# Queries of two chunks loaded as runs of eight tokens, and four re-orderings, in a fused linear-attention and feed-forward kernel

## The chip, the cores and the metric

The kernel runs on one core of a Trainium2 chip. The metric is the device time of one execution in microseconds (us), lower is better. Runs of the kernel before took 651.63 us (median of three; 650.90 and 653.96 are the other two). One more execution was recorded by the hardware profiler: it took 652.51 us, of which 650.7 us lie between its first and its last instruction (the span).

The engines named below are TensorE (PE for its matmuls, PEld for its weight loads), VectorE (DVE), ScalarE (ACT), GpSimd (POOL) and SyncE (SP). SP and POOL matter here mostly as queues from which DMA transfers are issued, in order.

## The reference

Two blocks in sequence, all in float32 (the inputs `moe_w_in`, `moe_w_out` arrive as 64-bit floats and are converted in the kernel):

```python
# attention: B=4, H=8, S=768, D=64, blocks of 64 tokens
for b in range(nb):
    intra = (qb @ kb.T * Dmask) @ vb
    inter = (qb * lam_pow) @ kv_state
    out[:, :, sl] = intra + inter
    kv_state = lam_block * kv_state + (kb * rev_pow).T @ vb
x = out.transpose(0, 2, 1, 3).reshape(3072, 512)
# feed-forward: d_ff = 2048
h = x @ w_in
g = h - tanh(h)
return g @ w_out
```

## The kernel before

**Groups and chunks.** The 768 tokens are cut into six groups `g` of 128 tokens; a group has four chunks `(g, b)`, one for each batch entry. For each group the kernel computes attention for its four chunks, then the first product `x @ w_in` with tanh (called "up", in four units `u` of 512 columns), then the second product (called "down"). Both products go by seven-product block schemes, the later ones twice nested, so they need sums and differences of weight blocks, called factors. Attention of the next group is woven between the products of the current one.

**Group 0, where the weights arrive too.** SP issues the loads of q, k and v and of the raw weights in one order. `load_natural` (lines 150 to 162) loads a chunk of q as `[token, head, d]` on 128 partitions, in pieces of 256 bytes (64 floats of one head). `att_transpose` (383) turns it on PE into a PSUM bank (`tp`), four 128x128 transposes for q and four for k, and copies each bank out (`qt`, `kt`) with one instruction, on ACT, or on DVE for k of chunks 2 and 3 of group 0. `first_scores` (409) makes eight score matmuls in two PSUM banks (`sp`) and masks them on DVE into `ss`; `first_decay` (421) scales k on DVE; `first_state` (454) makes the products `kv`; `first_out` (458) multiplies `ss` with v into two banks (`op`), from which `copy_xt` fills `xt`, the input of the first up-product (`h`, line 1044). All these PSUM tiles rotate through four banks with the tag "att". `weights` converts one raw weight block (`round_block`, lines 326 to 342: three ACT instructions at 337 to 339, then two DVE instructions at 341 and 342), and issues the loads of later blocks as it goes.

The order of group 0 and of the start of group 1 is written out by hand (lines 1108 to 1204). `tied(True, op)` and `keep_in_program_order` hold an instruction at its written place on its engine; the others are placed by a scheduler. The list `turns` (1163) weaves up-products of units 2 and 3 with conversions and with the attention of group 1; in its first entry one conversion stands in the middle of the up-product, ahead of `att_qd`, whose product `qd` (line 406) the next matmuls of PE (`op`, line 522) read. Then `down_first` (line 1074, tile `acc`) reads `s24`, sums made on DVE by `sums_late` (lines 1083, 1084), while DVE also builds factors (`sums_out`, 303; `sums_fine`, 321) and POOL issues their writes to DRAM.

**Group 1** (`second_units`, 1251). `pieces(g, at)` looks up in a table what attention work of the next group is done at this place; `att_scores` for chunks 0 and 1 stands under key 1. Its keys come from `turn_block` (line 373), a DVE transpose. `inner_weights` writes factors to the DRAM tensor `fine_in`.

**Groups 2 to 5** (`later_units`, 1268). The weight blocks of the twice nested products are streamed from the DRAM tensor `fine` through a ring of seven tiles `wb` (`piece`, 822; issued by POOL at line 843). In group 2 the last fourteen blocks of `fine` are still missing. `fine_factors(n)` (870), a generator for n = 1 and 2, loads four quarters of a factor (`f`, line 878), issues three DRAM-to-DRAM copies (880), and then, at each further step, one DVE difference (`hold`, shown at line 919) and the write of its result (885). `up` drives the steps of n = 2 at the tanh of the units and columns listed at line 680; `later_units` finishes the rest at line 1293.

Of the kernel before, what the change touches and what calls it, by code (L numbers as in the profile page):

```python
# [24 lines left out]
def kernel(  # L25
# [119 lines left out]

    raw, late = {}, {}
    chunks = [(g, b) for g in range(NG) for b in range(B)]
    at = {"loaded": 0}

    def load_natural(g, b, names):  # L150
        for name, src, bufs in (("q", q, 2), ("k", k, 4), ("v", v, 4)):
            if name in names:
                x = (qpool if name == "q" else io).tile([128, H, D], F32, name=f"{name}_nat", tag=name, bufs=bufs)
                if name == "q" or g == 0:
# [227 lines left out]

    def att_transpose(g, bs):
        for b in bs:
            load(g * B + b + 1)
            t = raw[g, b]
            qt = work.tile([128, NP, BLK], F32, name="qt", tag="qt")
            kt = work.tile([128, NP, BLK], F32, name="kt", tag="kt")
            for dst, x in ((qt, "q"), (kt, "k")):
                if g >= GB:  # L390
                    turn_block(dst, t[x + "b"])
# [17 lines left out]
    def first_scores(b):  # L409
        qt, kt, _ = tr[0, b]  # L410
        sp = [bank("sp", "att", 4).rearrange("s (p i) -> s p i", p=NP) for _ in range(2)]
        for p in range(NP):
            for j in range(2):
                tied(True, nc.tensor.matmul(out=sp[j][:, p, :], lhsT=kt[ts(j, 64), p, :], rhs=qt[ts(j, 64), p, :],
                                            start=True, stop=True))
# [3 lines left out]
        sc[0, b] = ss  # L419

    def first_decay(b):
        kp = raw[0, b]["k"].rearrange("s (p j) d -> s p j d", j=2)
        tied(True, nc.vector.tensor_tensor(kp, kp, bwd0, op=AL.mult))
# [34 lines left out]
    def first_out(bs):  # L458
        ops, dst = out_banks()
        for n, b in enumerate(bs):  # L460
            ss, vn = sc.pop((0, b)), raw[0, b]["v"]
# [5 lines left out]
        copy_xt(0, bs[0] // 2, ops)  # L467

    def score_products(g, b, tags):
# [183 lines left out]
    def up(g, u, n, wait=False, inside=False):  # L653
# [21 lines left out]
        def finish(c, src):  # L675
            th = work.tile([128, 2, HB], F32, name="th", tag="th")
            tied(g == 0, nc.scalar.activation(th, src, AF.Tanh))  # L677
            if g >= GI:
                pieces(g, ("t", u, c))
                if (u, c) in ((2, 12), (3, 12), (3, 22)):  # L680
                    next(made[g, 2], None)
# [186 lines left out]
    made = {}  # L868

    def fine_factors(n):  # L870

# [3 lines left out]
        for i in range(2):  # L875
            for j in range(2):
                t.append(late["pool"].tile([128, NU, 128], F32, name="f2", tag="sums", bufs=4))
                tc.keep_in_program_order(nc.gpsimd.dma_start(out=t[-1], in_=f[:, :, i, ts(j, 128)]))
        for x, i, j in ((0, 0, 0), (1, 1, 0), (2, 1, 1)):
            tc.keep_in_program_order(nc.gpsimd.dma_start(out=to[x], in_=f[:, :, i, ts(j, 128)]))  # L880
        yield
# [225 lines left out]

    for b in P0:
        att_transpose(0, (b,))
        first_decay(b)  # L1110
        first_scores(b)
    first_state(P0)
    half = up_plain(0, (11, 12))
    att_transpose(0, (2,))
    first_decay(2)
    weights(1)
    first_out(P0)
    first_scores(2)
    next(half)
# [4 lines left out]
    first_decay(3)  # L1124
    first_scores(3)
    next(half)
    first_state(P1)
    weights(KI + 1)
    first_out(P1)
    sums = first_sums()  # L1130
# [14 lines left out]
    for n in (2, 6, 5, 7):  # L1145
# [3 lines left out]
        if n == 6:  # L1149
# [12 lines left out]
    load(2 * B)  # L1162
    turns = [(2, (11, 21), 1, 1, (), ((att_transpose, 1, P0), (att_qd, 1, P0), (sums_in, 0))),
             (2, (12,), 0, 2, (), ((att_read, 1, P0), (att_scores, 1, P0, ("att", "att", "ya", "yb")))),
# [42 lines left out]
    def pieces(g, at_):  # L1207
# [43 lines left out]
    def second_units(g):  # L1251
        for u in range(NU):
            for n in (2, 6, 5, 7, 1, 4, 3):
# [137 lines left out]
```

## Time and profile before

| what | us |
|---|---|
| median of three runs | 651.63 |
| the profiled execution | 652.51 |
| its span | 650.7 |
| PE busy in the span | 639.8 |
| DVE busy | 497.8 |
| ACT busy | 239.2 |
| POOL busy | 225.4 |

The granted TensorE clock is at full speed in all forty slices of the span. The DMA engines moved 140.45 MB. Busy times by stage, from the view by windows:

| stage, us of the span | PE busy | DVE busy | ACT busy | DMA share |
|---|---|---|---|---|
| 0 to 25 (attention of group 0) | 21.63 | 16.44 | 11.06 | 0.99 |
| 25 to 61 | 35.97 | 30.62 | 28.59 | 0.86 |
| 61 to 127 (weights, factors) | 65.05 | 60.11 | 41.71 | 0.90 |
| 127 to 300 (groups 1 and half of 2) | 172.32 | 139.00 | 52.28 | 0.84 |
| 300 to 312 (products of group 2 begin) | 9.62 | 9.11 | 2.03 | 1.01 |
| 312 to 450 | 137.64 | 108.43 | 40.70 | 0.76 |
| 450 to 650.7 | 197.55 | 134.12 | 62.84 | 0.54 |

A DMA share is the mean busy share of sixteen DMA engines; it can pass 1 where packets overlap. Instructions on one engine run in order, so an engine's time line is read from top to bottom; a bracket behind a row gives the idle time ahead of it and what ended it. Matmul ends are modelled, so that the start-to-start distance of matmuls says more than their durations.

### The profile page before, as it was taken

The page shows a single profiled execution, that of the slowest core. Times are in us where ns is not written, and L with a number is a line of the kernel's source. Part 1 is how long each engine was busy: PE and PEld are TensorE (multiplying, and loading weights), DVE is VectorE, ACT ScalarE, POOL GpSimd, SP SyncE. Part 2 cuts the span into 40 slices and gives each one's busy share as a digit, 9 for nine tenths or more (in the row PEclk, how much of TensorE's full clock was granted, in tenths as well). Part 3 has the DMA queues.
Part 4 walks back from the last instruction along what each step waited for, and adds up shares of the span by engine and source line. Part 5 has one row for each costly group of instructions (what it writes and reads, how often), then busy time and mean ns, then how long its engine had stood idle before and what let it go on. Part 6 is the DMA issues. An engine that isn't in the chain of part 4 may idle for free.

```text
span 650.7 us, 14789 instructions
## 1 busy us (share of the span) xinstructions
PE 639.8 (98%) x5792; PEld 588.9 (90%) x5792; DVE 497.8 (77%) x902; ACT 239.2 (37%) x490; POOL 225.4 (35%) x392
## 2 busy tenths in 40 slices
PE   8999999999999999999999999999999999999998
PEld 7888888888888999888899988999988999988997
DVE  5879997987876967888868777878777878356583
ACT  3787773513322124442122353122344212444110
POOL 2001248782113554243555100646211456300440
PEclk9999999999999999999999999999999999999999
DMA  9979888999468877999979765778683587610582
GB/s 201 272 203 224 228 262 287 327 318 275 128 160 219 264 241 218 236 294 247 289 239 305 177 132 136 261 241 292 206 177 99 166 289 256 212 35 1 161 283 75
DMA packets 108789, 140.45 MB, mean 216 GB/s; under 512 B 64048, under 2 KB 81584, under 8 KB 108720
## 3 DMA queue, kind: packets, MB, share of 16 engines
q0 software_dynamic: 29840, 97.54, 47.1%
q1 hardware_dynamic: 78736, 41.96, 27.3%
q8 instruction: 46, 0.75, 0.5%
q14 instruction: 23, 0.19, 0.1%
q10 hardware_dynamic: 144, 0.00, 0.0%
HBM read 117.18 MB, written 23.86 MB: 217 GB/s over the span
## 4 chain that ended last, share of the span: by engine, by line
PE 70%; issue 10%; DMA 8%; DVE 7%; POOL 3%; SPq 1%; ACT 0%; POOLq 0%; DVEq 0%; ACTq 0%
PE y L961 15%; PE y L669 14%; PE zw L961 11%; PE z L669 5%; PE w L669 5%; PE y L767 4%; PE h L1044 3%; PE z L767 2%; DMA wb<-fine 2%; DMA fine<-f 2%; PE kv L449 1%; PE sp L486 1%; PE op L536 1%; DMA fine<-wt 1%; SPq L161 1%
## 5 line engine op out<-in xcount | busy, mean ns | idle before, releaser
L843 POOL DMA_DIRECT2D wb<-fine x217 | 117.1, 540 | 219.4 <-PE y L961 112.1
L961 PE MATMUL y<-wb,g 128*128 128x128 f32 x624 | 81.3, 276 | 0.6 <-DMA wb<-fine 0.5
L964 ACT ACTIVATE q<-y 128x128 f32<-128x128 f32 x108 | 30.0, 278 | 138.0 <-PE y L961 138.0
L961 PEld LDWEIGHTS y<-wb,g 128*128 128x128 f32 x624 | 75.3, 192 | 1.5 <-DVE ss L493 0.6
L961 PE MATMUL zw<-wb,g 128*128 128x128 f32 x416 | 55.2, 276 | 0.7 <-DMA wb<-fine 0.7
L961 PEld LDWEIGHTS zw<-wb,g 128*128 128x128 f32 x416 | 50.6, 192 | 1.0 <-PE y L961 0.6
L677 ACT ACTIVATE th<-g 128x512 f32<-128x512 f32 x42 | 26.5, 630 | 55.7 <-DVE g L700 20.8
L669 PE MATMUL y<-xt,w 128*128 128x256 f32 x200 | 46.9, 380 | 0.0
L1044 PE MATMUL h<-xt,w 128*128 128x256 f32 x192 | 44.1, 383 | 0.2 <-DVE w L342 0.2
L682 DVE TENSOR_TENSOR g<-g,th 128x512 f32<-128x512 f32 x42 | 29.0, 691 | 17.7 <-ACT th L677 17.5
L669 PEld LDWEIGHTS y<-xt,w 128*128 128x128 f32 x200 | 37.6, 190 | 5.1 <-ACT g L709 0.2
L1044 PEld LDWEIGHTS h<-xt,w 128*128 128x128 f32 x192 | 35.6, 190 | 5.7 <-DVE w L342 0.9
L669 PE MATMUL w<-xt,w 128*128 128x256 f32 x168 | 40.5, 383 | 0.0
L669 PE MATMUL z<-xt,ws 128*128 128x256 f32 x168 | 39.7, 379 | 0.0
L669 PE MATMUL y<-tt,w 128*128 128x256 f32 x160 | 38.1, 381 | 0.0
L669 PE MATMUL y<-tt,ws 128*128 128x256 f32 x160 | 38.1, 380 | 0.0
L669 PEld LDWEIGHTS z<-xt,ws 128*128 128x128 f32 x168 | 31.9, 190 | 4.3
L669 PEld LDWEIGHTS w<-xt,w 128*128 128x128 f32 x168 | 31.0, 190 | 4.5 <-ACT w L640 0.5
L961 PE MATMUL y<-wb,s 128*128 128x128 f32 x248 | 32.8, 275 | 1.5 <-DMA wb<-fine 1.5
L669 PEld LDWEIGHTS y<-tt,w 128*128 128x128 f32 x160 | 30.1, 190 | 4.3 <-DVE g L691 0.2
L669 PEld LDWEIGHTS y<-tt,ws 128*128 128x128 f32 x160 | 30.0, 190 | 3.9
L961 PE MATMUL zw<-wb,s 128*128 128x128 f32 x248 | 33.0, 276 | 0.0
(221 smaller groups left out, 1370.1 us busy)
## 6 DMA issues: line engine op xcount, KB each, us to landing
wb<-fine POOLq DMA_DIRECT2D x217, 256.0 KB, 3.8
fine<-f POOLq DMA_DIRECT2D x24, 256.0 KB, 4.7
wb<-fine_in POOLq DMA_DIRECT2D x24, 256.0 KB, 4.1
raw<-in_moe_w_out_dram POOLq DMA_DIRECT2D x10, 512.0 KB, 5.5
q_blk<-in_q_dram SPq DMA_DIRECT2D x32, 128.0 KB, 4.4
k_blk<-in_k_dram SPq DMA_DIRECT2D x32, 128.0 KB, 5.2
wb<-factors POOLq DMA_DIRECT2D x16, 256.0 KB, 4.5
raw<-in_moe_w_in_dram SPq DMA_DIRECT2D x7, 512.0 KB, 5.9
```

Of the source, the lines that this page charges most:

```text
L161: tc.keep_in_program_order(nc.sync.dma_start(out=x[rows, hs:hs + NP], in_=part.rearrange("h s d -> s h d")))
L449: tied(True, nc.tensor.matmul(out=kv[ts(j, 64), n, p, :], lhsT=kd[:, 2 * p + j, :], rhs=vn[:, 2 * p + j, :], start=n == 0 and p == 0, stop ...
L486: tied(True, nc.tensor.matmul(out=dst, lhsT=keys(p, j, late_), rhs=qt[ts(j, 64), p, rows], start=True, stop=True))
L536: tied(True, nc.tensor.matmul(out=dst(n, p, j)[:, HF:BLK], lhsT=vn[:, 2 * p + j, :], rhs=ss[:, j, p % 2, 1 + p // 2, :], start=first and n ...
L669: tied(g == 0, nc.tensor.matmul(out=t[:, m, :], lhsT=wt[:, kt, ts(m, 128)], rhs=x[:, kt, :], start=first and m == 0 and kt == 0, stop=kt = ...
L677: tied(g == 0, nc.scalar.activation(th, src, AF.Tanh))
L682: tied(g == 0 or g >= GI and inside, nc.vector.tensor_tensor(dst(c), src, th, op=AL.subtract))
L767: tied(True, nc.tensor.matmul(out=dst[:, ts(u, 128)], lhsT=a, rhs=b, start=x in (1, 2, 5) and u == 0, stop=True, skip_group_check=True))
L843: nc.gpsimd.dma_start(out=t.rearrange("p m c -> p (m c)"), in_=fine[TWICE.index(n_), SLOT.index(x_)].rearrange("p u c -> p (u c)"))
L961: tied(True, nc.tensor.matmul(out=dst, lhsT=a[:, u, :], rhs=wb[:, ts(u, 128)], start=x in begins and u == 0, stop=u == NU - 1, skip_group_ ...
L964: nc.scalar.activation(keep, dst, AF.Copy)
L1044: tied(u == 0 or u == 2 and cs[0] == 11, nc.tensor.matmul(out=hm[c][:, m, :], lhsT=w1[u][:, i, a, ts(m, 128)], rhs=xt[0, t][:, i, :], star ...
```

## The change

1. Chunks 0 and 1 of group 0 load q as runs of eight tokens: a partition holds eight consecutive tokens of one head, 2 KB in one piece. The transposes then take two tokens at a time, and four ACT copies of 64 partitions by 256 elements, with gaps in what they read and write, put the result in the layout of `qt`.
2. In the written order of group 0 the scores of chunk 0 are split in halves around the transposes of k of chunk 1, q of chunk 1 is transposed ahead of them, and the outputs of chunks 0 and 1 are parted by the transposes of k of chunk 2.
3. The conversion in the first entry of `turns` moves behind `att_qd`.
4. In group 1 the scores of chunks 0 and 1 for group 2 get places of their own, a little later.
5. The three DRAM-to-DRAM copies of each factor move from group 2 into group 1 (`fine_copies`), and the steps of n = 2 are driven from earlier places; the clean-up at the end of `later_units` goes.

```diff
+    RUNS = ((0, 0), (0, 1))
...
+                if name == "q" and (g, b) in RUNS:
+
+                    rows = src[b, 0, 0:BLK, :]
+                    rows = bass.AP(tensor=rows.tensor, offset=rows.offset, ap=[[8 * D, BLK // 8], [S * D, H], [1, 8 * D]])
+                    tc.keep_in_program_order(nc.sync.dma_start(out=x, in_=rows))
...
+    def runs_transpose(dst, x):
+
+        tp = bank("tp", "att", 4).rearrange("d (i c) -> d i c", i=4)
+        for i in range(4):
+            tied(True, nc.tensor.transpose(out=tp[:, i, :], in_=x[:, 2 * i:2 * i + 2, :], identity=ident))
+        dst = dst.rearrange("d p (t i e) -> d e i t p", i=4, e=2)
+        tp = tp.rearrange("d i (t p j) -> d j i t p", p=NP, j=2)
+        for j in range(2):
+            for e in range(2):
+                tied(True, nc.scalar.activation(dst[ts(j, 64), e], tp[ts(e, 64), j], AF.Copy))
...
         for p in range(NP):
+            if p == NP // 2:
+                yield
             for j in range(2):
...
-                if (u, c) in ((2, 12), (3, 12), (3, 22)):
+                if (u, c) in ((3, 11), (2, 12), (2, 21), (3, 12)):
                     next(made[g, 2], None)
...
+    def fine_copies(n):
+        f = factors[XAT[FACT[n][1]]].rearrange("p (u i) c -> p u i c", i=2)
+        for x, i, j in ((0, 0, 0), (1, 1, 0), (2, 1, 1)):
+            tc.keep_in_program_order(nc.gpsimd.dma_start(out=fine[TWICE.index(n)][x], in_=f[:, :, i, ts(j, 128)]))
...
-        for x, i, j in ((0, 0, 0), (1, 1, 0), (2, 1, 1)):
-            tc.keep_in_program_order(nc.gpsimd.dma_start(out=to[x], in_=f[:, :, i, ts(j, 128)]))
         yield
...
-    for b in P0:
-        att_transpose(0, (b,))
-        first_decay(b)
-        first_scores(b)
+    att_transpose(0, (0,))
+    first_decay(0)
+    att_transpose(0, (1,), "q")
+    scores = first_scores(0)
+    next(scores)
+    att_transpose(0, (1,), "k")
+    every(scores)
+    first_decay(1)
+    every(first_scores(1))
     first_state(P0)
     half = up_plain(0, (11, 12))
-    att_transpose(0, (2,))
+    att_transpose(0, (2,), "q")
+    outs_ = first_out(P0)
+    next(outs_)
+    att_transpose(0, (2,), "k")
     first_decay(2)
     weights(1)
-    first_out(P0)
-    first_scores(2)
+    every(outs_)
+    every(first_scores(2))
...
-    turns = [(2, (11, 21), 1, 1, (), ((att_transpose, 1, P0), (att_qd, 1, P0), (sums_in, 0))),
+    turns = [(2, (11, 21), 0, 1, (), ((att_transpose, 1, P0), (att_qd, 1, P0), (weights, 4 * KI + 1), (sums_in, 0))),
...
-            table.update({0: [(att_transpose, h, P0)], 1: [(att_scores, h, P0), (att_qd, h, P0)],
+            table.update({0: [(att_transpose, h, P0)], 1: [(att_qd, h, P0)], "6": [(att_scores, h, (0,))],
+                          "2": [(att_scores, h, (1,))],
                           2: [(att_transpose, h, (2,))], 3: [(att_transpose, h, (3,))]})
...
                     sums_in(u + 2)
+                if (u, n) in ((2, 6), (3, 2)):
+                    pieces(g, str(n))
             inner_weights(u, INNER if u + 1 < NU else INNER[1:])
+            if u < 2:
+                fine_copies(u + 1)
...
             if u == 0:
                 every(made[g, 1])
-            elif u == NU - 1:
-                every(made[g, 2])
```

The order in which the built program holds its instructions shows what this makes of each engine. On PE the first scores of chunk 0 stand behind the transposes of q of chunk 1, and the scores for group 2 stand one and three matmuls later than before. On ACT each of two `qt` copies becomes four, and the three conversion steps stand behind two tanh and four copies. On DVE the pair of conversion steps stands behind `qd`, and each of the four differences of n = 2 stands earlier. On POOL the six copies stand behind the `fine_in` writes of units 0 and 1 of group 1. On SP nothing but the shape of the two q loads changes.

More of the change, by code (lines that the diff above doesn't have):

```diff
@@ L153, in load_natural @@
                 x = (qpool if name == "q" else io).tile([128, H, D], F32, name=f"{name}_nat", tag=name, bufs=bufs)
-                if name == "q" or g == 0:
+                if name == "q" and (g, b) in RUNS:
+                    rows = src[b, 0, 0:BLK, :]
+                    rows = bass.AP(tensor=rows.tensor, offset=rows.offset, ap=[[8 * D, BLK // 8], [S * D, H], [1, 8 * D]])
+                    tc.keep_in_program_order(nc.sync.dma_start(out=x, in_=rows))
+                elif name == "q" or g == 0:
                     tc.keep_in_program_order(
@@ L381, in turn_blocks, with att_transpose @@
         turn_block(tr[g, b][x], raw[g, b]["qk"[x] + "b"])
-    def att_transpose(g, bs):
+    def runs_transpose(dst, x):
[7 more added lines that the diff above has]
+                tied(True, nc.scalar.activation(dst[ts(j, 64), e], tp[ts(e, 64), j], AF.Copy))
+    def att_transpose(g, bs, names="qk"):
         for b in bs:
@@ L386, in att_transpose @@
             t = raw[g, b]
-            qt = work.tile([128, NP, BLK], F32, name="qt", tag="qt")
-            kt = work.tile([128, NP, BLK], F32, name="kt", tag="kt")
+            qt = work.tile([128, NP, BLK], F32, name="qt", tag="qt") if "q" in names else tr[g, b][0]
+            kt = work.tile([128, NP, BLK], F32, name="kt", tag="kt") if "k" in names else None
             for dst, x in ((qt, "q"), (kt, "k")):
+                if x not in names:
+                    continue
+                if x == "q" and (g, b) in RUNS:
+                    runs_transpose(dst, t[x])
+                    continue
                 if g >= GB:
@@ L419, in first_scores @@
         sc[0, b] = ss
+        yield
     def first_decay(b):
@@ L460, in first_out @@
         for n, b in enumerate(bs):
+            if n:
+                yield
             ss, vn = sc.pop((0, b)), raw[0, b]["v"]
@@ L467, in first_out @@
         copy_xt(0, bs[0] // 2, ops)
+        yield
     def score_products(g, b, tags):
@@ L1124 @@
     first_decay(3)
-    first_scores(3)
+    every(first_scores(3))
     next(half)
@@ L1128 @@
     weights(KI + 1)
-    first_out(P1)
+    every(first_out(P1))
     sums = first_sums()
```

## The prediction

> **What bounds the kernel now.** First the page's busy times: PE holds the span, so only PE's idle time can be won.
>
> ```profile
> PE 639.8 (98%) x5792; PEld 588.9 (90%) x5792; DVE 497.8 (77%) x902; ACT 239.2 (37%) x490; POOL 225.4 (35%) x392
> ```
>
> 650.7 less 639.8 is 10.9 us. The view of waits, PE alone, says whom they were spent on (total us, times, longest):
>
> ```profile
> PE y L961 <- DMA wb<-fine: 1.9, 2, 1.5
> PE idle L363 <- POOL ident masks.py:199: 1.6, 1, 1.6
> PE sp L414 <- ACT kt L400: 1.4, 2, 0.7
> PE op L522 <- DVE qd L406: 0.8, 1, 0.8
> PE zw L961 <- DMA wb<-fine: 0.7, 2, 0.4
> PE sp L486 <- DVE kt L373: 0.5, 2, 0.3
> PE h L1044 <- DVE w L342: 0.2, 1, 0.2
> PE acc L1074 <- DVE s L1083: 0.2, 1, 0.2
> PE tp L395 <- DMA k_nat<-in_k_dram: 0.2, 1, 0.2
> ```
>
> The 1.6 us of the first row (before the first instruction can start) and some 3.2 us behind PE's last matmul stay. So at most about 6 us can go, and each part aims at a row. The time lines, PE unless the row says otherwise, give the places. The start:
>
> ```profile
> 6.19 0.66 PE L395 MATMUL tp<-ident,k_nat 128*128 128x128 f32 x4 [0.16 <-DMA k_nat<-in_k_dram]
> 7.54 1.16 PE L414 MATMUL sp<-qt,kt 64*128 64x128 f32 x16 [0.69 <-ACT kt L400]
> 10.46 1.16 PE L414 MATMUL sp<-qt,kt 64*128 64x128 f32 x16 [0.74 <-ACT kt L400]
> 19.00 0.48 PE L1044 MATMUL h<-xt,w 128*128 128x256 f32 x1 [0.20 <-DVE w L342]
> ...
> 6.07 0.60 ACT L400 ACTIVATE qt<-tp 128x512 f32<-128x512 f32 x1 [3.59 <-PE tp L395]
> 13.98 0.69 DVE L398 COPY kt<-tp 128x512 f32<-128x512 f32 x1 [0.44 <-ACT qt L400]
> ```
>
> PE waits twice for ACT's copies, and at 19.00 for DVE. Next, the first products of group 2, with POOL's queue:
>
> ```profile
> 306.56 1.13 PE L961 MATMUL y<-wb,g 128*128 128x128 f32 x8 [0.47 <-DMA wb<-fine]
> 308.12 1.13 PE L961 MATMUL zw<-wb,g 128*128 128x128 f32 x8 [0.43 <-DMA wb<-fine]
> 310.73 1.13 PE L961 MATMUL y<-wb,s 128*128 128x128 f32 x8 [1.48 <-DMA wb<-fine]
> ...
> 302.45 0.55 POOL L885 DMA_DIRECT2D fine<-f  x1
> ```
>
> A factor write stands in the queue between ring loads. Last, DVE in the stage from 61 to 127:
>
> ```profile
> 96.41 0.69 DVE L342 CUSTOM_DVE_ANT_0 wt<-wt,r 128x1024 uint16<-128x1024 uint16 x1 [0.67 <-ACT r L339]
> 109.32 0.69 DVE L321 TENSOR_TENSOR f<-wt,ws 128x512 f32<-128x512 f32 x1 [1.89 <-DMA fine<-f]
> 113.60 0.42 DVE L1083 TENSOR_TENSOR s<-gS,g 128x256 f32<-128x256 f32 x1
> ```
>
> DVE is busy 60.11 of 66 us there, and PE's `acc` at 114.07 starts 0.05 us after this sum ends: behind the PE rows there is a second limit.
>
> **The start (parts 1 and 2): 0.0, from -0.7 to +0.5.** A 256 KB load in 256-byte pieces lands 1.19 us after the one before it (k 6.15, q 7.33, k 8.54, v 9.74); raw weights of 256 KB in 2 KB pieces, 0.72 and 0.80 us. Two q loads so save some 0.9 us of queue, k of chunk 0 lands before q's transposes end, and 0.16 goes. But `qt` now costs four ACT copies of 256 elements. ACT rows: 128x128 takes 278 ns, 128x512 598, so 256 elements 385; successive copies start 0.115 us before the last one ends, so every 0.27. The q copies start at 6.07 as before (the warm-up matmuls hold PE until 4.95, so an earlier q wins 0.05 at most), the k copy ends at 6.07 + 4 x 0.27 + 0.60 = 7.75, and the scores start at 7.80, not 7.54. With k of chunk 1 between the halves (0.44) the masks start at 7.80 + 1.19 + 0.44, about 9.5 (before 8.73). Here DVE takes over: masks, decay and masks (1.21 + 0.60 + 1.29) end at 12.6, `op` of chunk 0 starts at 12.65 (it writes the banks just read), k of chunk 2 is turned behind it (0.85 + 0.73), and DVE's `kt` copy starts at 14.25. From that copy to the `h` at 19.00 DVE has 4.77 us without waits (19.00 - 13.98 - 0.25): 19.0, as before. The lower end: if this chain on DVE does not decide, PE alone is 0.5 us ahead at the scores of chunk 2 and the 0.20 goes too. The upper end: no row shows such a copy. Reading every second word, ACT L337 takes 670 for 598 ns; DVE's transpose takes 1.10 for 0.69. At 1.6 times per element a copy starts every 0.40 us, and four of them move the first scores by 0.5. I take the contiguous price, as L337 lies nearer to it.
>
> [...]
>
> **The conversion (part 3): -0.6, from 0 to -0.8.** `qd` stands behind a pair on DVE (0.42 + 0.69, with a gap 1.17 us). Moved, `qd` of chunk 0 is ready at about 60.5 and PE's `op` starts when its last `h` issues, 60.97, not 61.76: 0.79. The three ACT steps (2.0 us) then run behind four copies, done by 61.6, and the DVE pair follows `qd` at 61.1: `ws` starts at 62.2 as before, so DVE wins nothing here. POOL's raw load at 58.75, which waits for the steps' buffer, moves to 61.7, lands some 6.6 us later at 68.3, and is read by ACT at 69.50. DVE then runs on without gaps to 96.41, where it waits 0.67 us for ACT. That chain hangs on PE (ACT's `xt` copies at 79.76 and 91.62 wait for PE `op`), so it comes 0.7 earlier, and the wait can go. `acc` at 114.07 therefore keeps 0.6 of 0.79. The bounds: DVE gains nothing, or follows whole.
>
> **Scores (part 4): -0.54.** PE waits 0.22 at 170.06 and 0.32 at 180.97 for `kt`. One and three matmuls of 0.43 us go ahead instead; both waits are covered. DVE has 4 us of 10 idle behind it (190 to 200). Uncovered, it would be zero.
>
> **Copies and writes (part 5): -2.3, from -1.2 to -2.4.** Three waits make 2.38 us. Ring loads issued from 301.03 to 304.6 land 5.4, 6.1, 7.6, 8.1 and 8.2 us later, while seven tiles at 0.895 us each cover 6.3. From 262 SP's loads go out each as an earlier one lands, so the traffic ahead of 301 decides. Six copies land 0.72 to 0.80 us apart and all fall into 273 to 291: without them SP's last sixteen loads (294.4 to 304.6) come some 4 us earlier. The write at 302.45 waited for a DVE difference at 301.17; the four differences now go by 293, into DVE's idle stretches (1.18 us at 283.9). I take nearly all of it. The low end halves it. In group 1 the copies stand at about 163 and 176, where POOL has nothing else, the DMA share is 0.44 to 0.52, and the next user of a load (`qt` at 174.2, landed 168.2) has 6 us. What is late next: the first difference needs two `f` loads, landed at 286.75; at 283.9 they must have come 2.9 us earlier, of which the first three copies give 2.3. DVE may stand 0.6 us, PE's nearest reader of it (`z` at 290.38) has 0.67.
>
> **Sum:** 0.0 - 0.6 - 0.54 - 2.3 = -3.44 on the profiled execution's 652.51 (650.7 and 1.8 around the span): 649.07. The median shown lies 0.88 lower: 648.2.
>
> **Rivals**, in the runs' median.
>
> *The stall is halved and the conversion's gain is lost to DVE.* For it: ring loads take 8 us to land and DVE is full before 114. Against: the copies are 4.5 us of the traffic. 0 + 0 - 0.54 - 1.2 = -1.74: 649.9.
>
> *All PE rows go.* -0.7 - 0.79 - 0.54 - 2.38 = -4.41: 647.2. Against: DVE at 14 to 19.
>
> *Copies at twice the price per element.* A copy has 0.06 us that do not depend on its size (0.27 less 256 x 0.83 ns), so one starts every 0.06 + 0.43 = 0.49 us; the first scores start at 8.7, +0.9 at 19.00: -2.54, 649.1. For it: both sides of the copy have gaps. Against: L337 pays a fraction of it. [...]
>
> *Slower: the copies dearer still.* Place: ACT from 6.07 to the scores of chunk 1. With one every p us these start at 7.3 + 8p, and above p = 0.5 each 0.1 us costs 0.8. The gains elsewhere (3.44) are eaten at p = 0.8; at p = 1.3, nearly six times the contiguous rate, it is +7.3 - 3.44: 655.5. Against: no ACT row costs more than 1.12 times.
>
> **Chances.** Forecast 0.47, halved 0.17, all rows 0.20, twice the price 0.07, slower 0.09. A measurement can tell about 0.5%, 3.26 us: below 648.4 counts as faster, above 654.9 as slower. The forecast lies on that bound, 0.31 of its 0.47 beyond; with "all rows" 0.51. Slower takes 0.08 of the last rival, the same the other 0.41. The range: 647.2 less 1.2 for the scatter of three runs (650.90 to 653.96), 646.0; up to the halved case with 2.1 above, 652.0.
>
> **What would show it.** Right: no PE wait for `wb` near 306, no `sp` wait for DVE `kt`, none for `qd`; the `acc` wait for DVE sums grows by 0.1 to 0.3. PE's second `h` stands at 19.0. ACT rows of 64x256 at about 385 ns. Wrong: those at 500 ns or more, PE waits for `z` near 290, DVE standing at the first difference, ring loads still 7 us to landing at 303.

## The result and the profile after

The changed kernel takes 656.09 us (median of 13 runs, 652.79 to 658.87); the kernel before, run in turn with it on the same chip, 652.26 us (13 runs). The ratio is 1.0062, 95% interval 1.0044 to 1.0080: 2.9 to 5.2 us slower. The forecast was 648.2 in a range of 646.0 to 652.0, with 0.08 for slower. The profiled execution has a span of 654.4 us, 3.7 more than before. Two executions of the study, of 941.78 us (loads of queries only) and 1103.75 us (the kernel before), ran at mean granted clocks of 0.656 and 0.558 and are left out of every figure here.

The page of the changed kernel, busy times and the clock row of the slices:

```profile
PE 643.4 (98%) x5792; PEld 590.9 (90%) x5792; DVE 498.0 (76%) x902; ACT 242.4 (37%) x496; POOL 224.4 (34%) x392
...
PEclk8999999999999999999999999999999999999999
```

PE has the same 5792 matmuls and is busy 3.6 us longer (639.8 before); its idle time hardly changed. So the matmuls themselves got slower somewhere, and the first slice of the clock row says where. The waits of PE in the changed kernel (total us, times, longest):

```profile
PE y L697 <- DVE g L719: 1.9, 1, 1.9
PE sp L438 <- ACT kt L422: 1.7, 2, 1.3
PE idle L369 <- POOL ident masks.py:199: 1.6, 1, 1.6
PE h L1075 <- DVE w L348: 0.5, 1, 0.5
PE acc L1105 <- DVE s L1114: 0.4, 2, 0.2
PE tp L417 <- DVE ss L521: 0.4, 1, 0.4
PE tp L417 <- DMA k_nat<-in_k_dram: 0.4, 1, 0.4
PE y L992 <- ACT q L995: 0.3, 1, 0.3
```

Every row that the change aimed at in groups 1 and 2 is gone: no wait for `wb`, none of `op` for `qd`, none of `sp` for DVE's `kt`. In their place stand a new largest row, PE waiting for DVE's `g`, and a longer wait at the start, `sp` for ACT's `kt`. The start, first ACT, then PE (start, duration of the group, instructions, and in brackets the wait ahead of it):

```profile
6.43 2.63 ACT L398 ACTIVATE qt<-tp 64x256 f32<-64x256 f32 x4 [3.99 <-PE tp L393]
9.08 0.60 ACT L422 ACTIVATE kt<-tp 128x512 f32<-128x512 f32 x1
9.58 2.61 ACT L398 ACTIVATE qt<-tp 64x256 f32<-64x256 f32 x4
12.21 0.60 ACT L422 ACTIVATE kt<-tp 128x512 f32<-128x512 f32 x1
```

```profile
9.73 0.72 PE L438 MATMUL sp<-qt,kt 64*128 64x128 f32 x8 [1.28 <-ACT kt L422]
10.38 0.89 PE L417 MATMUL tp<-ident,k_nat 128*128 128x128 f32 x4
11.20 1.23 PE L438 MATMUL sp<-qt,kt 64*128 64x128 f32 x8
12.86 2.08 PE L438 MATMUL sp<-qt,kt 64*128 64x128 f32 x16 [0.43 <-ACT kt L422]
14.87 1.97 PE L474 MATMUL kv<-v_nat,k_nat 128*64 128x64 f32 x32
...
24.15 1.13 PE L1075 MATMUL h<-xt,w 128*128 128x256 f32 x4 [0.49 <-DVE w L348]
```

Four copies take 2.63 us, 0.66 each, and the four do not overlap: ACT is busy without a break from 6.43 to 12.8 and PE follows it. The second thing to see is the matmuls' own pace: eight `sp` take 0.72 us at 9.73 and 1.23 at 11.20; sixteen take 2.08 at 12.86, and took 1.16 before. The second `h`, at 19.00 before and forecast to stay there, is at 24.15. The view by windows gives the granted clock (columns: window, its length, busy us and instructions of PE, PEld, DVE, ACT, POOL, then the clock, the DMA share and GB/s):

```profile
7.25:10.66 3.41, 1.96 (x18) 1.37 (x18) 0.69 (x1) 3.35 (x6) 1.23 (x4) 1.00 1.36 216
10.66:17.49 6.83, 6.40 (x64) 5.43 (x62) 3.78 (x6) 2.10 (x4) 0.00 (x0) 0.50 1.23 262
```

For 6.83 us the clock is 0.50, right behind 3.41 us in which PE was busy for 1.96. In the kernel before the clock is 1.00 there.

The other loss is at 292 us, DVE first, then PE:

```profile
288.47 0.68 DVE L710 TENSOR_TENSOR g<-y,th 128x512 f32<-128x512 f32 x1
292.29 0.69 DVE L950 TENSOR_TENSOR f<-f,f 128x512 f32<-128x512 f32 x1 [3.14 <-DMA f<-factors]
```

```profile
294.24 1.99 PE L697 MATMUL y<-tt,w 128*128 128x256 f32 x8 [1.89 <-DVE g L719]
```

DVE stands 3.14 us for the first moved difference, whose loads have not landed, and PE 1.89 us for the `g` behind it. Then the ring, where the kernel before waited three times from 306.56 to 310.73:

```profile
307.09 1.05 PE L992 MATMUL y<-wb,g 128*128 128x128 f32 x8
307.98 1.06 PE L992 MATMUL zw<-wb,g 128*128 128x128 f32 x8
308.88 1.06 PE L992 MATMUL y<-wb,s 128*128 128x128 f32 x8
309.77 1.06 PE L992 MATMUL zw<-wb,s 128*128 128x128 f32 x8
```

One group starts 0.89 us after the other, without a wait.

Comparing the start of each matmul with that of the same matmul before tells where the 3.6 us of the profiled execution lie: +5.15 by 25 us, +0.63 from there to 140, -0.67 to 186, +0.16 to 286, +2.15 to 300, -3.51 to 317, -0.30 to the end; sum +3.61.

### The profile page after: what moved, and what is told of

Same layout as the page of the kernel before. It is cut to its first block, busy times and chain, and to the rows that moved or that the text cites. A ratio compares the mean times of both kernels' runs of the same rounds, so it can differ in the third digit from the quotient of the medians.

```text
span 654.4 us, 14786 instructions
## 1 busy us (share of the span) xinstructions
PE 643.4 (98%) x5792; PEld 590.9 (90%) x5792; DVE 498.0 (76%) x902; ACT 242.4 (37%) x496; POOL 224.4 (34%) x392
## 4 chain that ended last, share of the span: by engine, by line
PE 74%; DVE 10%; DMA 5%; ACT 5%; issue 3%; SPq 1%; POOL 1%; DVEq 0%; POOLq 0%; ACTq 0%
PE y L992 16%; PE y L697 15%; PE zw L992 12%; PE z L697 6%; PE w L697 5%; PE y L795 4%; DMA q_blk<-in_q_dram 2%; PE acc L1105 2%; PE y L927 2%; PE z L795 2%; PE sp L514 2%; PE op L564 1%; DMA fine<-f 1%; SPq L167 1%; PE op L550 1%
```

## The experiments

All ratios are to the kernel before, run in turn on the same chip, with the 95% interval. The steps are us gained (-) or lost in the one profiled execution, between the points of the kernel before that head the column. "Half clock" counts executions whose mean granted clock was below 0.998; by estimate, one stretch of 3.41 us at 0.50 makes 0.997 of a whole execution. The kernel before had 13 of 111.

| kernel | ratio | half clock | 0-25 | 25-140 | 140-186 | 186-286 | 286-300 | 300-317 | 317-640 |
|---|---|---|---|---|---|---|---|---|---|
| changed kernel | 1.0062 (1.0044-1.0080) | 8 of 13 | +5.15 | +0.63 | -0.67 | +0.16 | +2.15 | -3.51 | -0.30 |
| changed, no runs | 0.9995 (0.9973-1.0018) | 0 of 10 | +0.56 | +0.64 | -0.68 | +0.07 | +2.02 | -3.14 | +0.22 |
| before, runs alone | 1.0128 (1.0099-1.0157) | 4 of 4 | +7.05 | +0.04 | 0.00 | +0.07 | 0.00 | -1.70 | -0.19 |
| changed, differences later | 1.0037 (1.0022-1.0051) | 6 of 10 | +2.58 | +0.13 | -0.68 | +1.07 | 0.00 | -2.94 | +2.26 |
| changed, no runs, differences later | 0.9990 (0.9971-1.0009) | 0 of 10 | +0.60 | +0.16 | -0.68 | +1.67 | 0.00 | -3.51 | +1.08 |
| changed, PE kept busy | 1.0031 (1.0014-1.0047) | 2 of 7 | +3.44 | -0.06 | -0.68 | +1.55 | +0.91 | -3.51 | +0.72 |
| before, conversion alone | 0.9986 (0.9968-1.0004) | 0 of 10 | +0.37 | -0.07 | 0.00 | +0.89 | 0.00 | -1.35 | +0.85 |
| before, scores and copies, differences later | 0.9961 (0.9945-0.9977) | 0 of 9 | +0.31 | -0.11 | -0.68 | +0.06 | 0.00 | -0.64 | +2.89 |
| before, copies alone | 1.0006 (0.9990-1.0022) | 1 of 10 | +0.31 | -0.15 | 0.00 | +0.62 | +1.18 | -3.51 | +0.78 |
| before, copies of queries only | 1.0111 (1.0090-1.0133) | 4 of 4 | +6.88 | +0.20 | -0.01 | +0.41 | 0.00 | +0.10 | +1.04 |
| before, loads of queries only | 1.0012 (0.9989-1.0035) | 3 of 9 | +0.70 | +0.15 | 0.00 | +0.04 | 0.00 | -1.89 | +0.61 |
| changed, old start, differences later | 0.9964 (0.9946-0.9982) | 0 of 12 | +0.28 | +0.54 | -0.68 | 0.00 | 0.00 | -3.51 | +2.38 |
| changed, writes 8 bytes apart | 1.0013 (0.9997-1.0029) | 1 of 12 | +1.37 | +1.37 | -0.68 | +1.00 | +2.03 | -3.51 | +0.41 |
| before, copies, differences later | 0.9977 (0.9962-0.9993) | 0 of 12 | +0.09 | +0.75 | 0.00 | -0.28 | 0.00 | -3.51 | -0.32 |
| before, scores alone | 1.0000 (0.9981-1.0018) | 1 of 12 | +0.29 | +0.76 | -0.68 | -0.08 | 0.00 | -0.17 | +0.69 |
| changed, both mends | 0.9974 (0.9956-0.9991) | 0 of 12 | +1.33 | +0.77 | -0.68 | -0.07 | 0.00 | -3.51 | +0.72 |

The scatter of the steps is part of the reading. Six kernels in the table start exactly as the kernel before does, and their first step is +0.09 to +0.37; so a single first step within some 0.4 us says nothing.

**The start: are the runs to blame, or the new order?** The runs taken out of the changed kernel:

```
-    RUNS = ((0, 0), (0, 1))
+    RUNS = ()
```

> The changed kernel with the query loads of chunks 0 and 1 as runs undone (they are loaded token by token and turned by the ordinary eight-by-four path); the parted first scores and outputs, the new written order, the copies of the factors and the moved conversion stay. Theory: the start's 5.1 us come from the runs alone (each gapped copy of 64 rows by 256 holds ScalarE 0.65 us, TensorE starves and its granted clock falls to half from 10.7 to 17.5 us); so the offset to the kernel before falls from +5.2 to between -0.5 and +0.5 us at 25 us of the span, the granted clock stays whole there, and the time is about 651, some 5 us below the changed kernel, with the wait of 1.9 us at 294 us still in place. Rival: the new order (queries of chunk 1 turned ahead of the scores of chunk 0) itself starves TensorE and causes half or more of it; then +2.5 us or more stay at 25 us and the time is 653.5 or more.

The 0-25 step falls from +5.15 to +0.56, no execution has the half clock, and the time falls by 0.67% (4.4 us); the two intervals do not meet. The runs alone in the kernel before (the load branch and `runs_transpose` of the change, in the old order):

> The kernel before with the query loads as runs (and the copies that go with them) alone; the old order. Theory: the offset at 25 us is +4 to +6 us and the time that much above the kernel before, 656 to 658, since the copies and the lost clock come with the runs whatever the order. Rival (the new order is what costs): within 1.5 us of the kernel before. What the new order is worth is this run against the changed kernel's +5.2.

+7.05, more than expected and worse than in the changed kernel, with the clock halved twice in the profiled execution (9.44 to 12.85 and 16.27 to 19.68). PE waits 2.35 us there for the first scores, and 1.28 in the changed kernel, where the turned queries of chunk 1 come first. So the runs make the loss, and the new order eases it. Without the runs the new order's step of +0.56 is some 0.3 above the +0.09 to +0.37 of kernels with the old start.

**Loads or copies?** The two halves of the runs, each alone in the kernel before; first the turning without the loads:

> The kernel before with the turning of the query runs for chunks 0 and 1 alone (four copies of 64 rows by 256, read from every second number, written to steps of 512 bytes); the queries are loaded token by token as before, so the first two chunks' scores come from queries in another order of tokens, which changes no amount of work. Theory: the copies alone make the loss; they start some 0.4 us earlier than in the changed kernel since the loads land as before: 4 to 7 us above the kernel before, with each copy 0.63 to 0.66 us, one behind the other. Rival: it is the loads in pieces of 2 KB, which hold up those behind them; then within 1 us of the kernel before.

+6.88: the copies are the loss. Then the loads with the ordinary turning (`pass` in place of `runs_transpose`, so that the eight-by-four path follows):

> The kernel before with the query loads of chunks 0 and 1 as runs alone, and the ordinary turning (the first two chunks' scores come from queries in another order of tokens). Theory: the loads land 0.2 to 0.5 us later than token by token, and TensorE follows them: +0.3 to +0.8 us at 25 us and in the time. Rival (the prediction's step for the loads): they land sooner or as before, 0 to -0.7 us.

+0.70 in the trace; the time alone (1.0012) cannot tell it from nothing. The first keys land at 6.68 us (6.15 before), the queries of chunk 1 at 7.74 (7.33), their keys at 8.90 (8.54), and the first queries themselves at 5.19 (4.96). Of these four loads none comes sooner with pieces of 2 KB for the queries; they come 0.2 to 0.5 later.

**Which side of the copy costs?** Eight copies of 64x256 with other steps on either side, in a kernel that ran once:

> The copies as in the run of the copies of queries only, with other steps in each of the eight (64 rows by 256 each; most of them put the queries of chunks 0 and 1 in wrong places). Chunk 0: first read and written without gaps; second read from every second number, written without gaps; third read without gaps, written as in the change (numbers one behind another 512 bytes apart); fourth read and written as in the change. Chunk 1: first as in the change; the others the same numbers in another order, written 32 bytes apart (second, third) and 8 bytes apart (fourth). Theory, from 0.65 us against some 0.385 worked out for 256 numbers without gaps: the price lies on the writing side, so chunk 0 gives 0.39, 0.39, 0.65, 0.65, and the last of chunk 1 is nearer to 0.39 since it writes 8 bytes apart. Rival: it lies in reading every second number out of PSUM: 0.39, 0.65, 0.39, 0.65 and all of chunk 1 at 0.65. A second rival: each gap costs its half: 0.39, 0.52, 0.52, 0.65.

The time line of ACT in that kernel:

```profile
6.25 2.08 ACT L411 ACTIVATE qt<-tp 64x256 f32<-64x256 f32 x4 [3.77 <-PE tp L390]
8.36 0.60 ACT L433 ACTIVATE kt<-tp 128x512 f32<-128x512 f32 x1
10.79 2.32 ACT L411 ACTIVATE qt<-tp 64x256 f32<-64x256 f32 x4 [1.84 <-PE tp L390]
```

and its eight copies one by one (ns, start to start where another copy follows):

```
chunk  read from PSUM       written to SBUF      took   to next start
0      one by one           one by one           377    390
0      8 bytes apart        one by one           381    392
0      one by one           512 bytes apart      641    653
0      8 bytes apart        512 bytes apart      646
1      8 bytes apart        512 bytes apart      647    659
1      32 bytes apart       32 bytes apart       631    642
1      32 bytes apart       32 bytes apart       619    631
1      512 bytes apart      8 bytes apart        391
```

The theory holds in every row. Reading at 8 or at 512 bytes costs at most 0.014 us; writing costs as little at 8 bytes and some 0.25 us per copy at 32 and at 512. And a copy of 64x256 starts 0.39 us after the one before even without gaps: it does not overlap as the 128x512 copies do, of which the next starts after 0.50 of 0.60 us (9.32 and 9.82 us in the kernel before). Where between 8 and 32 bytes the price of writing sets in, and why, is not shown.

**The same numbers at the lower price.** With that, the changed kernel's copies can be written in another order:

```
-        dst = dst.rearrange("d p (t i e) -> d e i t p", i=4, e=2)
-        tp = tp.rearrange("d i (t p j) -> d j i t p", p=NP, j=2)
+        dst = dst.rearrange("d p (t i e) -> d e p t i", i=4, e=2)
+        tp = tp.rearrange("d i (t p j) -> d j p t i", p=NP, j=2)
```

> The changed kernel with the same numbers copied in another order: each of the eight copies writes 8 bytes apart (and reads 512 bytes apart) in place of writing 512 bytes apart (and reading 8). Same work, same results. Theory: a copy takes 0.39 us in place of 0.65, so the four take 1.6 us in place of 2.6; the keys of chunk 0 are ready 1.1 us sooner and TensorE's wait of 1.28 us at 9.7 us nearly goes; the clock stays whole. The offset at 25 us falls from +5.15 to between +1 and +2 us, and the time is 2 to 4 us below the changed kernel, ratio to the kernel before 1.000 to 1.003. Rival: the loss is set by the loads that land 0.3 to 0.4 us later and by the order, and the clock falls as before; then no more than 1 us is won, 1.005 or more.

ACT and PE there:

```profile
6.47 1.65 ACT L398 ACTIVATE qt<-tp 64x256 f32<-64x256 f32 x4 [4.03 <-PE tp L393]
8.14 0.60 ACT L422 ACTIVATE kt<-tp 128x512 f32<-128x512 f32 x1
8.64 1.60 ACT L398 ACTIVATE qt<-tp 64x256 f32<-64x256 f32 x4
10.26 0.60 ACT L422 ACTIVATE kt<-tp 128x512 f32<-128x512 f32 x1
```

```profile
8.79 0.71 PE L438 MATMUL sp<-qt,kt 64*128 64x128 f32 x8 [0.31 <-ACT kt L422]
9.44 0.66 PE L417 MATMUL tp<-ident,k_nat 128*128 128x128 f32 x4
10.02 0.72 PE L438 MATMUL sp<-qt,kt 64*128 64x128 f32 x8
10.91 1.16 PE L438 MATMUL sp<-qt,kt 64*128 64x128 f32 x16 [0.17 <-ACT kt L422]
```

1.65 us for four copies, a wait of 0.31 in place of 1.28, sixteen `sp` in 1.16 us again. The 0-25 step is +1.37 and the ratio 1.0013: 3.2 us won by the order of writing alone. Of the 24 executions that wrote 8 bytes apart (this kernel and the last of the table), 1 has the half clock; of the 23 that wrote 512 bytes apart in the new order (the changed kernel and the one with later differences), 14.

**How much of it is the clock?** The run with later differences (below) has the same start, and its profiled execution kept the whole clock: +2.58 against +5.15. Of these 2.57 us, 0.50 are there before the clock falls (the first scores start at 9.23 and 9.73 us), so the halved clock is some 2.1 us of the 5.15 in the profile. The times give less: the 8 executions of the changed kernel at half clock took 1.3 us longer on average than the other 5, and with later differences 6 took 1.2 us longer than the other 4. Whether the clock falls differs from execution to execution. One run tried to keep it up by six idle products in the wait:

```
+    for _ in range(6):
+        tied(True, nc.tensor.matmul(out=idle[:, 0:128], lhsT=ident, rhs=ident, start=True, stop=True))
```

> The changed kernel with six more 128x128 products into the scratch bank of the opening, put between the turned queries of chunk 1 and the scores of chunk 0; nothing else differs and they write to nothing that is read. They lie in TensorE's wait of 1.28 us at 9.7 us (six at 0.105 us are 0.63). Theory: of the 5.15 us lost by 25 us, 4.0 are longer matmuls and 1.1 more idle time; the long matmuls come from the granted clock falling to half after a stretch of 3.41 us with TensorE mostly idle, so with the products in the wait the clock stays whole and the offset at 25 us falls to between +1.5 and +3 us (the changed start ran at whole clock in the run with later differences: +2.6). The time is 1.5 to 3 us below the changed kernel where that one drew the half clock, 654. Rival: the clock falls whatever lies there, since the copies still space the matmuls out; the time is that of the changed kernel, 656, or more by the 0.63 us of the products.

2 of 7 executions had the half clock, and the profiled one kept it whole; the time is 2.0 us below the changed kernel, with intervals that just overlap. 2 of 7 against 8 of 13 can be chance, so it is not shown that the products keep the clock up. They hold PE for 1.50 us, not 0.63, but end as the keys are ready and delay nothing. The step of +3.44, above what was expected, comes from the first queries: they land at 5.83 us in this execution, 5.23 in the changed kernel.

In the four traces that have drops at the start, they came in whole stretches of 3.41 us at a clock of 0.50. That PE is mostly idle for 3.41 us ahead of a drop, as the expectation had it, holds in the old order, where it was busy for 0.63 to 0.95 us of these stretches, but not in the changed kernel, where it was busy for 1.96; and in the run with later differences a stretch with as little brought no drop:

```profile
8.53:11.94 3.41, 1.95 (x20) 1.47 (x20) 0.73 (x2) 3.33 (x7) 0.01 (x1) 1.00 1.33 218
```

The clock is 1.00 there and in the stretch behind it. What decides between these two stays open.

**The differences.** All four triggers one step later in the changed kernel:

```
-                if (u, c) in ((3, 11), (2, 12), (2, 21), (3, 12)):
+                if (u, c) in ((2, 12), (2, 21), (3, 12), (3, 22)):
```

> The changed kernel with the four triggers of the differences each one step later: (2,12), (2,21), (3,12), (3,22) in place of (3,11) first. Theory: VectorE's 3.14 us of standing at 292 us, and TensorE's 1.89 us at 294 us, come because the first difference is asked for before its factors have landed; asked for one step later they have landed, so the 1.89 us goes, the gain between 300 and 315 us (3.5 us) stays, and the time is about 2 us below the changed kernel, 654. Rival: the wait only moves to the next place where VectorE is needed, or the fourth difference now comes too late for the products that read it; then the time stays within 0.7 us of the changed kernel.

The step at 286-300 goes from +2.15 to 0.00, and the time falls by 0.25% (1.6 us) against the changed kernel, with intervals that just overlap; about 2 was expected. In its profile 2.26 us came back after 317 us, 1.5 of it idle in three waits for landings of weight blocks. The copies of the factors alone, with the change's triggers:

> The kernel before with the copies of the factors moved and the four triggers of the change (the first difference at (3,11)), nothing else. Theory: VectorE stands for the first difference at some 289 us as in the changed kernel, since the loads it reads are held up by the writes of the copies ahead of them in the same queue: TensorE loses 1.8 to 2.2 us there; the ring then gives 3.1 to 3.5 us back; net -1 to -1.7 us, 650.5 to 651.3. Rival (the prediction's step): the difference waits at most 0.6 us and the whole is -2.3, 650.0; or the wait at 289 us was due to the late start of the changed kernel and does not show here.

The wait shows (+1.18) with the old start too, so it is not a matter of the late start. The time is that of the kernel before, 1.0006, a miss: the 1 to 1.7 us expected lie outside the interval. The same with the later triggers:

> The kernel before with the copies of the factors moved and the differences one step later; nothing else. The prediction sized this at -2.3 us. Theory: with the trigger of the change it gave 1.0006 (its 0.9 to 2 us of VectorE's standing at 289 us eat the gain); one step later that is gone: 0.9965 to 0.998, -1.3 to -2.3 us. Rival: the ring's wait of 2.38 us in the one profile of the kernel before is not there in most executions (other profiles with the old copies have 0.9 to 1.9), so the gain is half of it or less, 0.998 to 1.000.

0.9977, 0.5 to 2.5 us faster. PE's waits there:

```profile
PE idle L363 <- POOL ident masks.py:199: 1.6, 1, 1.6
PE sp L414 <- ACT kt L400: 1.4, 2, 0.7
PE acc L1077 <- DVE s L1086: 0.8, 2, 0.4
PE op L522 <- DVE qd L406: 0.8, 1, 0.8
PE sp L486 <- DVE kt L373: 0.5, 2, 0.3
PE h L1047 <- DVE w L342: 0.2, 1, 0.2
```

Neither the new wait for `g` nor one for `wb` is among them.

**Scores and conversion, each alone in the kernel before.**

> The kernel before with the scores of the second group parted alone (first chunk after piece 6 of turn 2, second after piece 2 of turn 3). The prediction sized this at -0.54 us. Theory: -0.68 us at 186 us as in all profiles that have it, with nothing lost later; 0.999, -0.7 us. Rival: the 0.68 us are taken back by the ring at 306 us, as TensorE only reaches the same wait sooner: 1.000, and the wait there grows by 0.7 us.

The 0.68 us at 170 to 186 are there, and 0.67 or 0.68 in all ten profiles with this part; the time, 1.0000 within 0.2%, neither shows nor excludes them.

> The kernel before with the moved conversion alone (the stage opens at its piece 0 rather than 1, and one conversion of weights runs in the turn before). Theory from four traces with it in: 1.03 us are gained by 64 us (the wait of 0.79 us for qd goes, and 0.24 us of slow matmuls behind it) and 0.9 to 1.5 us are given back by 115 us, by a wait of 0.36 us of the transposes for the masked scores at 70 us and by accumulations whose matmuls run slower, with waits for the DVE sums; net -0.1 to +0.5 us, so the time is that of the kernel before within 0.5 us. Rival (the prediction's step): it keeps 0.6 us.

1.03 us are won by 64 us and 0.79 lost again by 115 us. The time (0.9986) leaves between 2.1 us faster and 0.3 slower. The step 25-140 has a mean of +0.46 us in the nine profiles with the conversion, and of +0.23 in the seven others: in the profiles nothing of the 1.03 is left by 140 us.

**The parts put together.** The changed kernel without runs and with later differences:

> The two edits together: no runs, and the differences one step later. Theory: the effects add (different parts of the span, one path): some 7 us below the changed kernel and 3.5 to 5 us below the kernel before, 647 to 649. Rival: part of the gain around 300 us exists only because the path there was late in the changed kernel; then it is 650 or more.

0.9990: a miss; 647 to 649 was expected. In its trace the two steps did add (0.00 and -3.51), but 1.67 us were lost by 286 us, most of it in one wait of 1.22 us at 247 us. There ACT's `r` waits until an output write of POOL's queue has landed, with the copy that PE needs behind it. The same code in the run without runs issued that write at the same time (240.47 against 240.51) and had it landed at 245.12 in place of 246.24, so this wait differs between executions. One trace does not explain a median of ten, though: why the time missed stays open. Then two kernels with the start of the kernel before, the first with its conversion as well:

> The parted scores of the second group and the copies of the factors at their new place, with the differences one step later; the start and the conversion are those of the kernel before. Theory: the step of 0.68 us at 186 us and that of 3.5 us around 306 us stay, nothing is lost at the start or by 115 us; 4 us below the kernel before, 648, unless the waits for landings (0.2 to 1.4 us in single profiles at 250 and at 425 us, where the queue runs just ahead of TensorE) take a part of it: then 649 to 651. Rival: what is gained around 306 us is always lost again by 440 us, since the queue of pieces and not TensorE sets the time from there; then within 0.5 us of the kernel before but for the 0.7 us of the scores.

> The changed kernel with the start as in the kernel before (no runs, the old order) and the differences one step later; the conversion, the parted scores of the second group and the copies of the factors as changed. Theory: what the run without start and conversion gave (ratio 0.9961, some 2.5 us) plus what the conversion gave alone (0.9986, within its interval of nothing): 0.995 to 0.997, 649.5 to 651. It stands 0.2 to 0.4% below the run that has the new order too (0.999): the new order costs 0.5 us in each trace by 25 us. Rival: the conversion takes back what the copies gain; 0.998 or more.

0.9961 and 0.9964, 1.2 to 3.6 us faster than the kernel before: the lowest ratios of the study, and without the new start. The profiled execution of the first was the longest of its nine runs and shows how the ring can fail even with the copies moved:

```profile
PE y L992 <- DMA wb<-fine: 2.0, 3, 1.0
PE zw L992 <- DMA wb<-fine: 1.6, 3, 0.7
```

SP's last block load was issued at 302.41 us and landed at 309.50, among the ring loads from 300.62 on; in the copies' run with later differences SP had issued its last by 299.54. Last, both mends in the changed kernel:

> The changed kernel with both mends: the copies write 8 bytes apart, and the differences come one step later. Theory: the effects add: what the other order of writing gains (2 to 4 us) and what the later differences gain (1.6 us): ratio to the kernel before 0.997 to 1.000. Rival: TensorE runs up to the queue of pieces by 250 us and by 440 us and stands there, and no more than the first mend shows, 1.000 to 1.003.

0.9974: the change as drawn up, with another order of writing and another place of four triggers, is 0.6 to 2.9 us faster than the kernel before. Its interval overlaps those of the three other kernels that are clearly faster, so which of the four is best is not shown.

## Why the prediction was wrong

**The start: the step that failed.** It was forecast at 0.0, and measured +5.15 us by 25 us. "ACT rows: 128x128 takes 278 ns, 128x512 598, so 256 elements 385; successive copies start 0.115 us before the last one ends, so every 0.27." The 385 is right for a copy written without gaps (377 and 381 measured), the overlap is not: 128x512 copies do overlap by 0.10, but two copies of 64x256 start 0.39 us apart. "I take the contiguous price, as L337 lies nearer to it" is the larger error: L337 reads with gaps, and these copies write with gaps, 512 bytes apart; that side costs 0.25 us per copy. So 0.66 us from copy to copy, not 0.27. The profile before had nearer rows than L337 (the view by lines: count, then busy us and mean ns, then idle us):

```profile
L338 ACT ACTIVATE r<-raw 128x512 int16<-128x512 uint32 x26 | 20.3, 780 | 7.3 <-DVE wt L342 7.3
L339 ACT ACTIVATE r<-raw 128x512 f16<-128x512 f32 x26 | 19.9, 765 | 0.0
```

Both read every second word and write 2-byte numbers 4 bytes apart, and they take 1.30 and 1.28 times the 598 ns. So "no ACT row costs more than 1.12 times" was not so. They change the number format too, so they do not show by themselves that the writing costs it; and no row had these copies' form, as the prediction said.

The prediction's last rival had the right place. That rival's own formula, the scores of chunk 1 at 7.3 + 8p, gives 12.6 us with p = 0.66; they came at 12.86, and at 12.36 where the clock stayed whole. By its prices (+0.9 us at p = 0.49, 0.8 for each 0.1 above 0.5) the second `h` comes some 2.2 us late; +2.58 was measured with the whole clock. So the path was seen, and the size of p was wrong. Its break-even at p = 0.8 was too high for two reasons: the clock, which no case had, and the gains, which were smaller than counted.

**What follows from PE starved: not foreseen at all.** Some 2.1 of the 5.15 us are the halved clock. A wait at 9 us was priced as its own length; it cost that much more where the clock fell (1.2 to 1.3 us by the mean times).

**The loads of the start.** "Two q loads so save some 0.9 us of queue": they save nothing; the keys behind them land 0.4 to 0.6 us later.

**The conversion, -0.6.** The wait for `qd` went as forecast (0.79, and 0.24 more that came with it), but behind DVE none of it was left: the transposes wait 0.4 us for the masked scores, `acc` for DVE's sums. That half of the rival "the conversion's gain is lost to DVE" was right.

**The scores, -0.54.** Right in the trace, where it is -0.67, as a wait costs more than its idle time; the times do not show it.

**The copies and writes, -2.3: right in kind, sized on one execution, and with a wrong side condition.** The waits at the ring go: 2.38 us of idle time in the profile before, and with what a wait costs beyond that, 3.51 us in eight of the eleven profiles. But the kernel before in its profile stood longer than usual: in six profiles of other kernels with the copies unmoved the same stretch is 0.8 us shorter on average. Measured end to end with later differences, the part is worth 1.5 us (0.5 to 2.5), which does not exclude the 2.3. "What is late next" named the right wait and priced it at 0.6 us, since "the first three copies give 2.3" of the 2.9 us by which the factors' loads had to come sooner. POOL's queue in the changed kernel shows why they gave nothing:

```profile
284.12 0.54 POOL L916 DMA_DIRECT2D fine<-f  x1 [1.81 <-DVE g L719]
284.65 2.28 POOL L911 DMA_DIRECT2D f<-factors  x3
289.35 0.75 POOL L911 DMA_DIRECT2D f<-factors  x1 [2.43 <-DMA fine<-f]
```

The loads stand behind the four writes of the factor before, and those wait for DVE; the copies were never in the way. In the kernel before the first two loads go out at 279.65 and 280.41 and land at 285.01 and 286.75; here at 284.65 and 285.40, landing at 290.47 and 292.17: 5.0 to 5.5 us later, as everything is there (5.3). The trigger was moved one step ahead, the data were not.

**The sum.** In the profiled executions the forecast was -3.44 and the result +3.61. Of these 7.05 us the start is 5.15; the stretch of the conversion adds 1.2, that of the copies and writes 1.1, and the rest takes 0.4 back. So the start is most of the miss; of what was forecast, the conversion gave nothing and the copies about half.

**Open.** What the new order costs without the runs: 0.3 us more than the old start in the traces (+0.56 and +0.60 against +0.09 to +0.37), while the times differ by 0.26% (0.9990 against 0.9964), their intervals overlapping. How often the ring's waits come in the kernel before was not counted beyond seven profiles. And what makes the clock fall in one execution and not in the next, and whether more work for PE prevents it, is not shown.

## What to carry to other kernels

Price a strided copy by the row that has its gaps on the same side: here the written side decided, and exchanging the loops of the access pattern, so that numbers are written 8 bytes apart in place of 512, won 3.2 us for nothing. Early in a kernel, add to a wait of the matmul engine the chance that its clock is halved: here it was in 8 of 13 executions of the changed kernel, and no later wait, of up to 1.9 us, brought that in any profile. When a consumer is moved ahead, follow its data back to the instruction that issues the load and what stands before that in its queue; taking other traffic away moves only what was waiting for traffic.

## What the runs showed of the hardware

- ScalarE, 64x256 float32 from PSUM to SBUF: 0.38 us written contiguously, 0.38 to 0.43 written 8 bytes apart, 0.62 to 0.65 at 32 or 512 bytes; reading steps of 8 and 512 bytes cost at most 0.014 us.
- Successive copies of 64x256 written contiguously start 0.39 us apart (0.63 to 0.66 at 32 or 512 bytes), their whole duration; a copy of 128x512 lets the next start after 0.50 of its 0.60.
- The granted clock fell to 0.50 for stretches of 3.41 us near the start; in 8 of 13 executions of one kernel, and in 8 of 8 where the copies stood in the old order.
- Loads of 256 KB in pieces of 2 KB, among the first of this kernel, landed no sooner than in pieces of 256 bytes (5.23 against 4.96 us for the first).
- A wait of PE cost more than its idle time. Behind the wait of 1.89 us at 294 us in the changed kernel the matmuls come another 0.27 us later: otherwise they overlap by 0.16 (0.38 us each, one every 0.22), and the first one behind the wait lasts 0.48.
